# Wide products, fewer TensorE instructions: a two-layer decode kernel on one Trainium2 core

## Chip, cores and metric

The kernel runs on one core of one Trainium2 chip. The metric is the device time of one execution in microseconds. Times are given as the median of several runs; the profile comes from one further execution.

## What is computed

Two layers run one after the other over the same weights. Each layer is a decode step of grouped-query attention over a key and value cache, and then a gated feed-forward block; both have a layernorm ahead and a residual sum behind. There are 4 batch rows of 512 numbers, 32 query heads on 8 key/value heads, 4096 cached positions with 128 numbers a head, and a hidden width of 1792. All numbers are f32.

```python
def _A_ref(x, k_cache, v_cache, wq, wo):          # B, Sq, D = 4, 1, 512; 32 heads on 8
    q = (x @ wq).reshape(B, Sq, Hq, Dh).transpose(0, 2, 1, 3)
    k = jnp.repeat(k_cache, rep, axis=1)
    v = jnp.repeat(v_cache, rep, axis=1)
    p = softmax(einsum("bhqd,bhkd->bhqk", q, k) * Dh ** -0.5)
    o = einsum("bhqk,bhkd->bhqd", p, v)
    return o.transpose(0, 2, 1, 3).reshape(B, Sq, Hq * Dh) @ wo

def _B_ref(x, w1, w3, w2):
    h = silu(x @ w1) * (x @ w3)
    return h @ w2

for layer in range(2):
    x = x + _A_ref(layernorm(x), k_cache, v_cache, wq, wo)
    x = x + _B_ref(layernorm(x), w1, w3, w2)
```

## The kernel before, in words

Every layer reads the whole cache, 64 MB of keys and 64 MB of values, so the program is mostly a stream of loads. The order of the loads is a list made ahead (`plan`, lines 120 to 187), and a small allocator gives each load a place in one large on-chip tile, `space`. `pump` (L192) issues the next loads of the list, all on SyncE's queue, as long as a place is free. `done` and `vacate` (L231, L240) return a place once TensorE has used what lay there, and call `pump` again. So a load is issued when TensorE has consumed something that came much earlier, and the loads land in the order of the list.

The attention walks over 16 steps in a layer: 8 key/value heads ("groups"), each in two halves of 2048 positions. `score` (L351) multiplies q with 16 key blocks of 512 positions. `maximum` and `exponent` make the softmax of one half with its own maximum (VectorE, ScalarE). `turn` (L379) transposes the weights p. `weigh` (L403) multiplies them with the value tiles. The blocks of scores and values run on four separate groups of 32 output partitions: `ps[32 * b:32 * b + 32, :]`. The work is interleaved: the scores of the next half are issued before the values of this half.

At the end of a group, `finish` (L413) joins the two halves. `join_sums` (L395) makes the factors of the halves, two instructions at L425 add them up into `o` (128 partitions by 4 blocks of 128 columns, of which each row needs one), and `turn_o` (L429) turns the four blocks in four products with parts of the identity. `project_o` (L437) multiplies by the group's 512 rows of wo: for each of the 4 heads of the group, four products of 128 columns, each into its own 32 partitions of `x_ps`; L448 adds the result to the residual `x_sb`. `project_q` (L329) makes the next group's q the same way: four row blocks of wq times four heads, 16 products of 128 columns into `misc[32 * h:32 * h + 32, :]`, one VectorE scaling (L344), one transposition (L345) and two copies into `qT`.

A product of f32 numbers is two TensorE instructions with a weight load each, a transposition is one.

The residual is held as four blocks of 128 columns, each on the first 4 rows of its own 32 partitions, which is why the projections write their output in four parts.

At the end of a layer, the last group's projection is followed by `layernorm` (L302), the products with w1 and w3 (L466, L460), the gate (L471 to L478), the turning of the hidden vector (`turn_h`, L480), and `down` (L499), the products with the 14 row tiles of w2: for each tile four products of 128 columns into `x_ps` (L504). w2 arrives in seven loads (`W2_PARTS`, tiles 0-1, 2-5, 6-7, 8-9, 10-11, 12, 13). The sum is added to `x_sb` at L520 or, in the last layer, at L523, and L562 stores the output. Between these steps the kernel issues work for TensorE whose result nobody reads: `busy(n)` (L287) transposes the identity n times; the list `BUSY` says how often at which place.

Of the kernel before, what the change touches and what calls it, by code (L numbers as in the profile page):

```python
# [52 lines left out]


W2_PARTS = ((0, 2), (2, 6), (6, 8), (8, 10), (10, 12), (12, 13), (13, 14))
BUSY = (5, 3, 5, 3, 3, 4, 3, 2)
SCRATCH = 64


# [4 lines left out]
def tile_decode_layers(ctx: ExitStack, tc: tile.TileContext, x, kt, v, wqo, wo0, w1, w3, w2, out):  # L64
# [192 lines left out]

    alike = const.tile([P, P], F32, name="alike")
    block = const.tile([P, 2 * NB], F32, name="block")
    part = work.tile([P, 48], F32, name="part", tag="tmp", bufs=1)  # L260
    nc.vector.tensor_reduce(part[:, 0:16].rearrange("p (b h) -> p b h", b=B),
                            ident.rearrange("p (b j h) -> p b h j", b=B, h=REP), axis=AX.X, op=ALU.add)
    for j in range(2 * NB):
        nc.vector.tensor_copy(alike.rearrange("p (b j h) -> p b j h", b=B, h=REP)[:, :, j, :],
                              part[:, 0:16].rearrange("p (b h) -> p b h", b=B))
    nc.vector.tensor_reduce(part[:, 16:48].rearrange("p (b j) -> p b j", b=B),
                            ident.rearrange("p (b j h) -> p b j h", b=B, h=REP), axis=AX.X, op=ALU.add)
    nc.vector.tensor_reduce(block, part[:, 16:48].rearrange("p (b j) -> p j b", b=B), axis=AX.X, op=ALU.add)
    qT = const.tile([P, B, 32 + LEAD], F32, name="qT")
    nc.vector.memset(qT, 0.0)  # L270
    oT = const.tile([P, REP, B], F32, name="oT")
    hT = const.tile([P, 14, B], F32, name="hT")
    sums_ps = psum.tile([P, 2, P], F32, name="sums_ps")
    nc.vector.memset(sums_ps, 0.0)
    x_ps, misc = sums_ps[:, 0, :], sums_ps[:, 1, :]
    o_ps = [psum.tile([P, NB * DH], F32, name=f"o{i}", tag=f"o{i}") for i in range(STEPS)]
    for i in range(STEPS):
        nc.vector.memset(o_ps[i], 0.0)

    def scores():  # L280
        return psum.tile([P, BLOCK], F32, name="scores", tag="scores")
# [4 lines left out]

    def busy(n):  # L287
        if n:
            pt = scores()
            for i in range(n):  # L290
                nc.tensor.transpose(pt[:, 0:P], ident, ident)  # L291

    def small(name, bufs=1):
        return work.tile([P, 1], F32, name=name, tag=name, bufs=bufs)
# [31 lines left out]
        return xT, rstd, factor  # L326


    def project_q(layer, g, xT, rstd, factor=None):  # L329
        w = place(at_wq(g), HOME).rearrange("p (k n) -> p k n", k=KC)  # L330

        def product(k):
            for h in range(REP):
                nc.tensor.matmul(misc[32 * h:32 * h + 32, :], xT[:, 32 * k:32 * k + 32],  # L334
                                 w[:, k, h * DH:(h + 1) * DH], start=(k == 0), stop=(k == KC - 1))

        for k in range(KC):
            product(k)
            if factor and k == 1:
                factor()  # L340
        if layer:
            vacate(at_wq(g))
        q = work.tile([P, DH], F32, name="q", tag="tmp", bufs=1)
        nc.vector.tensor_scalar(q, misc, rstd, SCALE, op0=ALU.mult, op1=ALU.mult)  # L344
        nc.tensor.transpose(misc, q, ident)  # L345
        for at in (LEAD, LEAD + ROW):
            nc.vector.tensor_copy(qT[:, :, at:at + REP],
                                  misc.rearrange("p (h b) -> p b h", h=REP)[:, 0:B, :])


    def score(layer, g, c):  # L351
# [43 lines left out]
    def join_sums(acc):  # L395
        nc.vector.tensor_tensor(acc[:, 8:10], acc[:, 2:4], acc[:, 4:6], op=ALU.mult)
        nc.vector.tensor_tensor(acc[:, 10:11], acc[:, 8:9], acc[:, 9:10], op=ALU.add)  # L397
        nc.tensor.matmul(misc[:, 8:9], alike, acc[:, 10:11], start=True, stop=True)  # L398
        nc.vector.reciprocal(acc[:, 11:12], misc[:, 8:9])
        nc.vector.tensor_scalar(acc[:, 12:14], acc[:, 4:6], acc[:, 11:12], 2.0, op0=ALU.mult, op1=ALU.mult)  # L400


    def weigh(layer, g, c, i, pT):  # L403
# [6 lines left out]
            done("v", layer, g, c, r)  # L410


    def finish(layer, g, c, i, p, acc, after=None):  # L413
        pT = turn(p)
        if i < STEPS - 1:
# [7 lines left out]
        for j in (0, 2):  # L423
            s = slice(j * DH, (j + 2) * DH)
            nc.vector.scalar_tensor_tensor(o[:, s], o_ps[1][:, s], acc[:, 13:14], o[:, s], op0=ALU.mult,  # L425
                                           op1=ALU.add)
        return o

    def turn_o(o):  # L429
        for j in range(NB):  # L430
            own = ident.rearrange("p (b j h) -> p b j h", b=B, h=REP)[:, :, j, :]
            nc.tensor.matmul(misc[:, 0:B * REP], o[:, j * DH:(j + 1) * DH], own,  # L432
                             start=(j == 0), stop=(j == NB - 1))
        nc.vector.tensor_copy(oT, misc[:, 0:B * REP].rearrange("p (b h) -> p h b", b=B))


    def project_o(layer, g, rowsum):  # L437
        w = place(at_wo(g), HOME) if g or layer == 0 else loaded("wo", layer)
        w = w.rearrange("p (h e) -> p h e", h=REP)
        for h in range(REP):  # L440
            for k in range(KC):
                nc.tensor.matmul(x_ps[32 * k:32 * k + B, :], oT[:, h, :], w[:, h, k * P:(k + 1) * P],  # L442
                                 start=(h == 0), stop=(h == REP - 1))
        if layer and g == 0:
            done("wo", layer)
        elif layer or g == 0:
            vacate(at_wo(g))
        nc.vector.scalar_tensor_tensor(x_sb, x_ps, 1.0, x_sb, op0=ALU.mult, op1=ALU.add,  # L448
                                       accum_out=rowsum)

    def feed_forward(layer, xT, rstd, factor, rowsum):
        pg = o_ps[0]
# [46 lines left out]
        def down():  # L499
            for i, (a, b) in enumerate(W2_PARTS):  # L500
                t = loaded("w2", layer, a).rearrange("p (n e) -> p n e", n=b - a)
                for m in range(a, b):
                    for k in range(KC):
                        nc.tensor.matmul(x_ps[32 * k:32 * k + B, :], hT[:, m, :],  # L504
                                         t[:, m - a, k * P:(k + 1) * P], start=(m == 0), stop=(m == 13))
# [21 lines left out]
    for layer in range(LAYERS):  # L527
        xT, rstd, factor = layernorm(x_sb, rowsum)
        steps = orders[layer]
        project_q(layer, steps[0][0], xT, rstd, factor)  # L530
        accs, before = {}, None
        for n, (g, c) in enumerate(steps):
            i = n % STEPS
            if i == 0:
                accs[g] = work.tile([P, 16], F32, name="acc")
            ps = score(layer, g, c)
            maximum(i, ps, accs[g])
            if n == 0:
                p = exponent(i, ps, accs[g])
            elif i == 0:  # L540
                o = finish(layer, *before, p, accs[before[0]])
                turn_o(o)
                p = exponent(i, ps, accs[g])
            else:
                if n > 1:
                    project_o(layer, steps[n - 2][0], small("rowsum"))
                p = finish(layer, *before, p, accs[g], (i, ps, accs[g]))
# [12 lines left out]
        rowsum = small("rowsum")  # L560
        feed_forward(layer, xT, rstd, factor, rowsum)
# [45 lines left out]
```

## Time and profile before

| | |
|---|---|
| median of 3 runs | 711.88 us (711.68 to 711.91) |
| the profiled execution | 712.09 us |
| its span, first to last instruction | 710.2 us |
| granted TensorE clock, mean | 0.817 |
| loads | 299.18 MB, 16 DMA engines busy 99.1% of the span |
| TensorE instructions | 3994 matmuls and 3994 weight loads |

The profile shows one execution. An instruction's row has its start and duration, its engine (PE is TensorE, PEld its weight loads, DVE VectorE, ACT ScalarE, POOL GpSimd, SPq the issuing of loads by SyncE), its line, what it writes and reads, its shape and how many of the same kind were merged into the row (x32). Brackets give the idle time of the engine ahead of it and what ended that. The chain of waits is followed back from the last instruction, at each step to what released it. Matmuls overlap, so a row of several is read by the starts of the rows around it rather than by summing durations.

### The profile page before, as it was taken

To read this page: it belongs to the slowest core of one execution; us is meant where nothing else is said; L and a number is where in the kernel's file an instruction comes from. 1 tells how busy PE (TensorE), PEld (TensorE's weight loads), DVE (VectorE), ACT (ScalarE), POOL (GpSimd) and SP (SyncE) were. 2 spreads that over 40 slices of the span, in tenths; PEclk is the share of its full clock that TensorE was granted. 3 is DMA by queue.
4 is the path that set the end of the run, shared out by engine and by line. 5 is a ranking of instruction groups with operands and counts; after the bars stand their busy time and mean duration, and the time that the engine had idled before them with its cause. 6 is when DMAs were issued, how large, how long until landed. Compare 5 with 4: busy or idle time off the path is not lost.

```text
span 710.2 us, 8882 instructions
## 1 busy us (share of the span) xinstructions
PE 452.9 (64%) x3994; PEld 166.2 (23%) x3994; DVE 106.5 (15%) x372; ACT 42.3 (6%) x101; POOL 2.9 (0%) x10
## 2 busy tenths in 40 slices
PE   4542766367662666675687766576566686666887
PEld 2111222122211222121234211122122222222234
DVE  2011011011110111111211110110111111111121
ACT  0000000000000000010111100000000000000011
POOL 0000000000000000000000000000000000000000
PEclk8687687677976889799999988886888867787799
DMA  9999999999999999999999999999999999999996
GB/s 374 434 436 431 426 435 429 430 433 427 435 430 432 433 427 429 434 418 418 420 419 408 412 426 429 428 433 432 430 435 425 431 437 420 438 426 424 426 417 257
DMA packets 19477, 299.80 MB, mean 422 GB/s; under 512 B 2160, under 2 KB 2416, under 8 KB 6384
## 3 DMA queue, kind: packets, MB, share of 16 engines
q1 hardware_dynamic: 19296, 299.18, 99.1%
q8 instruction: 31, 0.51, 0.3%
q10 hardware_dynamic: 144, 0.07, 0.0%
q14 instruction: 6, 0.05, 0.0%
HBM read 299.17 MB, written 0.07 MB: 421 GB/s over the span
## 4 chain that ended last, share of the span: by engine, by line
DMA 83%; PE 15%; DVE 1%; issue 1%; SPq 0%; ACT 0%; POOL 0%; ACTq 0%
DMA space<-in_v 47%; DMA space<-in_kt 28%; DMA space<-in_w 8%; PE scores L361 6%; PE o L408 6%; PE sums_ps L442 0%; PE scores L291 0%; PE sums_ps L334 0%; ACT p L375 0%; DVE acc L371 0%; SPq L213 0%; PE o L460 0%; SPq L201 0%; PE sums_ps L432 0%; PE sums_ps L504 0%
## 5 line engine op out<-in xcount | busy, mean ns | idle before, releaser
L408 PE MATMUL o<-space,pT 128*16 128x512 f32 x1024 | 170.1, 806 | 128.6 <-DMA space<-in_v 127.0
L361 PE MATMUL scores<-space,qT 128*32 128x512 f32 x1024 | 157.2, 763 | 81.0 <-DMA space<-in_kt 75.0
L408 PEld LDWEIGHTS o<-space,pT 128*16 128x16 f32 x1024 | 32.6, 117 | 235.2 <-issue 141.3
L361 PEld LDWEIGHTS scores<-space,qT 128*32 128x32 f32 x1024 | 41.0, 134 | 173.2 <-issue 140.6
L371 DVE TENSOR_REDUCE acc<-scores 128x1 f32<-128x512 f32 x32 | 22.1, 692 | 231.1 <-PE scores L361 231.1
L375 ACT ACTIVATE p<-scores,acc 128x512 f32<-128x512 f32 x32 | 22.0, 687 | 456.9 <-PE sums_ps L432 297.9
L425 DVE SCALAR_TENSOR_TENSOR o<-o,acc,o 128x256 f32<-128x256 f32 x32 | 14.0, 479 | 129.9 <-PE o L408 129.9
L392 DVE TENSOR_REDUCE acc<-sums_ps 128x1 f32<-128x8 f32 x16 | 2.7, 166 | 142.8 <-PE sums_ps L391 142.8
L432 PE MATMUL sums_ps<-ident,o 128*128 128x16 f32 x128 | 17.0, 265 | 8.6 <-DVE o L425 8.6
L334 PE MATMUL sums_ps<-space,xT 128*32 128x128 f32 x512 | 19.2, 294 | 3.7 <-DVE acc L392 3.6
L432 PEld LDWEIGHTS sums_ps<-ident,o 128*128 128x128 f32 x128 | 15.5, 191 | 25.3 <-DVE o L425 25.1
L382 PE MATMUL turned<-ident,p 128*128 128x128 f32 x128 | 21.0, 286 | 0.0
L442 PE MATMUL sums_ps<-space,oT 128*4 128x128 f32 x512 | 17.7, 280 | 0.0
L382 PEld LDWEIGHTS turned<-ident,p 128*128 128x128 f32 x128 | 13.6, 142 | 16.9 <-issue 16.0
L442 PEld LDWEIGHTS sums_ps<-space,oT 128*4 128x4 f32 x512 | 14.2, 90 | 10.1 <-issue 9.4
L291 PE MATMUL scores<-ident 128*128 128x128 f32 x80 | 14.6, 300 | 1.4 <-POOL ident masks.py:199 1.4
L334 PEld LDWEIGHTS sums_ps<-space,xT 128*32 128x32 f32 x512 | 13.9, 117 | 5.7 <-DVE acc L392 4.9
L398 PE MATMUL sums_ps<-acc,alike 128*128 128x1 f32 x32 | 6.1, 261 | 13.0 <-DVE acc L397 13.0
L384 DVE COPY pT<-turned 128x256 f32<-128x256 f32 x32 | 13.4, 419 | 4.3 <-PE turned L382 4.3
L393 ACT ACTIVATE acc<-acc 128x2 f32<-128x2 f32 x16 | 4.7, 296 | 144.6 <-DVE acc L392 144.6
L421 DVE TENSOR_SCALAR o<-o,acc 128x512 f32<-128x512 f32 x16 | 12.0, 751 | 0.6
L291 PEld LDWEIGHTS scores<-ident 128*128 128x128 f32 x80 | 9.5, 151 | 6.4 <-issue 4.9
(78 smaller groups left out, 141.5 us busy)
## 6 DMA issues: line engine op xcount, KB each, us to landing
space<-in_kt SPq DMA_DIRECT2D x23, 4096.0 KB, 28.3
space<-in_v SPq DMA_DIRECT2D x22, 4096.0 KB, 32.3
space<-in_v SPq DMA_DIRECT2D x11, 2048.0 KB, 22.0
space<-in_kt SPq DMA_DIRECT2D x9, 2048.0 KB, 19.7
space<-in_v SPq DMA_DIRECT2D x14, 1024.0 KB, 19.8
space<-in_wqo SPq DMA_DIRECT2D x3, 4096.0 KB, 42.7
space<-in_kt SPq DMA_DIRECT2D x7, 1024.0 KB, 11.8
space<-in_w SPq DMA_DIRECT2D x6, 1024.0 KB, 17.2
```

The source lines that it names most:

```text
L291: nc.tensor.transpose(pt[:, 0:P], ident, ident)
L334: nc.tensor.matmul(misc[32 * h:32 * h + 32, :], xT[:, 32 * k:32 * k + 32], w[:, k, h * DH:(h + 1) * DH], start=(k == 0), stop=(k == KC - 1))
L361: nc.tensor.matmul(ps[32 * b:32 * b + 32, :], qT[:, b, at:at + 32], t[:, i * BLOCK:(i + 1) * BLOCK], start=(m < 2), stop=(m >= TILES - 2))
L371: nc.vector.tensor_reduce(acc[:, i:i + 1], ps, axis=AX.X, op=ALU.max, negate=True)
L375: nc.scalar.activation(p.rearrange("p n s -> p (n s)"), ps, AF.Exp, bias=acc[:, i:i + 1], accum_out=acc[:, 2 + i:3 + i])
L382: nc.tensor.transpose(pt[:, n, :], p[:, n, :], ident)
L384: nc.vector.tensor_copy(pT, pt.rearrange("p n (b r) -> p n b r", b=B)[:, :, :, 0:ROW])
L408: nc.tensor.matmul(o_ps[i][32 * b:32 * b + ROW, :], pT[:, r // 2, b, :], t[:, j * NB * DH:(j + 1) * NB * DH], start=(r < 2), stop=(r >= TI ...
L421: nc.vector.tensor_scalar(o, o_ps[0], acc[:, 12:13], None, op0=ALU.mult)
L425: nc.vector.scalar_tensor_tensor(o[:, s], o_ps[1][:, s], acc[:, 13:14], o[:, s], op0=ALU.mult, op1=ALU.add)
L432: nc.tensor.matmul(misc[:, 0:B * REP], o[:, j * DH:(j + 1) * DH], own, start=(j == 0), stop=(j == NB - 1))
L442: nc.tensor.matmul(x_ps[32 * k:32 * k + B, :], oT[:, h, :], w[:, h, k * P:(k + 1) * P], start=(h == 0), stop=(h == REP - 1))
```

## The change

The parts of the change are:

- `project_q` uses, for all groups but a layer's first, four products of 512 columns into the first 32 partitions of a tile `wide` (the whole bank of `sums_ps`) in place of 16 products of 128 columns. The scaling becomes four instructions, one for each head. In the first group of a layer the order changes: `factor`, which makes rstd, is issued ahead of all products instead of after half of them. One copy into `qT` replaces two.
- `project_o` does the same for all groups but a layer's last: four products of 512 columns into 4 rows of `wide`. The result is added to the residual by `add_rows`, four VectorE instructions of 4 rows by 128 columns, which `finish` issues after the transposed weights were copied.
- The end of a group: `o` has one block of 128 columns instead of four. `join_sums` makes eight factors, one for each half and block, which are zero where a row doesn't own the block; one scaling and seven additions of 128 columns gather `o`. Four of these additions stand after the second half's values. `turn_o` is one product.
- `down`: the first ten tiles of w2 use one product of 512 columns each, into 4 rows of `sides[0]`; `add_rows` adds them to the residual. The last four tiles stay as they were.
- `busy(n)` issues one product of n times 128 columns in place of n transpositions, and the counts go from 5, 3, 5, 3, 3, 4, 3, 2 to 4, 3, 4, 3, 0, 4, 3, 2.

Matmuls and weight loads together go from 7988 to 6148.

```diff
-BUSY = (5, 3, 5, 3, 3, 4, 3, 2)
+WIDE = 10
+BUSY = (4, 3, 4, 3, 0, 4, 3, 2)
...
+    head = const.tile([P, B * REP], F32, name="head")
...
-    sums_ps = psum.tile([P, 2, P], F32, name="sums_ps")
+    sums_ps = psum.tile([P, KC, P], F32, name="sums_ps")
...
+    wide = sums_ps.rearrange("p k c -> p (k c)")
...
     def busy(n):
         if n:
-            pt = scores()
-            for i in range(n):
-                nc.tensor.transpose(pt[:, 0:P], ident, ident)
+            pt = scores().rearrange("p (k c) -> p k c", k=KC)
+            nc.tensor.matmul(pt[:, 0:n, :], ident, ident.unsqueeze(1).to_broadcast([P, n, P]),
+                             start=True, stop=True)
...
+        if factor:
+            factor()
         for k in range(KC):
-            product(k)
-            if factor and k == 1:
-                factor()
+            if factor:
+                for h in range(REP):
+                    nc.tensor.matmul(misc[32 * h:32 * h + 32, :], xT[:, 32 * k:32 * k + 32],
+                                     w[:, k, h * DH:(h + 1) * DH], start=(k == 0), stop=(k == KC - 1))
+            else:
+                nc.tensor.matmul(wide[0:32, :], xT[:, 32 * k:32 * k + 32], w[:, k, :],
+                                 start=(k == 0), stop=(k == KC - 1))
...
+            for h in range(REP):
+                nc.vector.tensor_scalar(q[32 * h:32 * h + 32, :], wide[0:32, h * DH:(h + 1) * DH],
+                                        rstd[0:32, :], SCALE, op0=ALU.mult, op1=ALU.mult)
...
+        nc.vector.tensor_tensor(acc[:, 16:24].rearrange("p (i j) -> p i j", i=2),
+                                block[:, 0:NB].unsqueeze(1).to_broadcast([P, 2, NB]),
+                                acc[:, 12:14].unsqueeze(2).to_broadcast([P, 2, NB]), op=ALU.mult)
...
-        o = work.tile([P, NB * DH], F32, name="o", tag="p", bufs=1)
-        nc.vector.tensor_scalar(o, o_ps[0], acc[:, 12:13], None, op0=ALU.mult)
+        o = work.tile([P, DH], F32, name="o", tag="p", bufs=1)
+        nc.vector.tensor_scalar(o, o_ps[0][:, 0:DH], acc[:, 16:17], None, op0=ALU.mult)
+
+        def add(s, js):
+            for j in js:
+                nc.vector.scalar_tensor_tensor(o, o_ps[s][:, j * DH:(j + 1) * DH], acc[:, 16 + NB * s + j:17 + NB * s + j],
+                                               o, op0=ALU.mult, op1=ALU.add)
+
+        add(0, range(1, NB))
         weigh(layer, g, c, i, pT)
...
+        add(1, range(NB))
...
     def turn_o(o):
...
+        nc.tensor.matmul(misc[:, 0:B * REP], o, head, start=True, stop=True)
...
+            if rowsum is None:
+                nc.tensor.matmul(wide[0:B, :], oT[:, h, :], w[:, h, :], start=(h == 0), stop=(h == REP - 1))
...
+    def add_rows(a):
+        for k in range(KC):
+            rows = x_sb[32 * k:32 * k + B, :]
+            nc.vector.tensor_tensor(rows, a[0:B, k * P:(k + 1) * P], rows, op=ALU.add)
...
+                    if m < WIDE:
+                        nc.tensor.matmul(sides[0][0:B, :], hT[:, m, :], t[:, m - a, :],
+                                         start=(m == 0), stop=(m == WIDE - 1))
...
+                if b == WIDE:
+                    add_rows(sides[0])
```

More of the change, by code (lines that the diff above doesn't have):

```diff
@@ L259, in tile_decode_layers @@
     block = const.tile([P, 2 * NB], F32, name="block")
-    part = work.tile([P, 48], F32, name="part", tag="tmp", bufs=1)
-    nc.vector.tensor_reduce(part[:, 0:16].rearrange("p (b h) -> p b h", b=B),
+    head = const.tile([P, B * REP], F32, name="head")
+    part = work.tile([P, 32], F32, name="part", tag="tmp", bufs=1)
+    nc.vector.tensor_reduce(head.rearrange("p (b h) -> p b h", b=B),
                             ident.rearrange("p (b j h) -> p b h j", b=B, h=REP), axis=AX.X, op=ALU.add)
@@ L410, in weigh, with finish @@
             done("v", layer, g, c, r)
-    def finish(layer, g, c, i, p, acc, after=None):
+    def finish(layer, g, c, i, p, acc, after=None, projected=False):
         pT = turn(p)
+        if projected:
+            add_rows(wide)
         if i < STEPS - 1:
@@ L419, in finish, with project_o @@
         join_sums(acc)
-        o = work.tile([P, NB * DH], F32, name="o", tag="p", bufs=1)
-        nc.vector.tensor_scalar(o, o_ps[0], acc[:, 12:13], None, op0=ALU.mult)
+        o = work.tile([P, DH], F32, name="o", tag="p", bufs=1)
[5 more added lines that the diff above has]
+        add(0, range(1, NB))
         weigh(layer, g, c, i, pT)
[L423 to L426, printed above, removed]
+        add(1, range(NB))
         return o
     def turn_o(o):
[L430 to L433, printed above, removed]
+        nc.tensor.matmul(misc[:, 0:B * REP], o, head, start=True, stop=True)
         nc.vector.tensor_copy(oT, misc[:, 0:B * REP].rearrange("p (b h) -> p h b", b=B))
-    def project_o(layer, g, rowsum):
+    def project_o(layer, g, rowsum=None):
         w = place(at_wo(g), HOME) if g or layer == 0 else loaded("wo", layer)
@@ L440, in project_o @@
         for h in range(REP):
-            for k in range(KC):
-                nc.tensor.matmul(x_ps[32 * k:32 * k + B, :], oT[:, h, :], w[:, h, k * P:(k + 1) * P],
-                                 start=(h == 0), stop=(h == REP - 1))
+            if rowsum is None:
+                nc.tensor.matmul(wide[0:B, :], oT[:, h, :], w[:, h, :], start=(h == 0), stop=(h == REP - 1))
+            else:
+                for k in range(KC):
+                    nc.tensor.matmul(x_ps[32 * k:32 * k + B, :], oT[:, h, :], w[:, h, k * P:(k + 1) * P],
+                                     start=(h == 0), stop=(h == REP - 1))
         if layer and g == 0:
@@ L447, in project_o @@
             vacate(at_wo(g))
-        nc.vector.scalar_tensor_tensor(x_sb, x_ps, 1.0, x_sb, op0=ALU.mult, op1=ALU.add,
-                                       accum_out=rowsum)
+        if rowsum is not None:
+            nc.vector.scalar_tensor_tensor(x_sb, x_ps, 1.0, x_sb, op0=ALU.mult, op1=ALU.add,
+                                           accum_out=rowsum)
+    def add_rows(a):
+        for k in range(KC):
+            rows = x_sb[32 * k:32 * k + B, :]
+            nc.vector.tensor_tensor(rows, a[0:B, k * P:(k + 1) * P], rows, op=ALU.add)
     def feed_forward(layer, xT, rstd, factor, rowsum):
@@ L534, in tile_decode_layers @@
             if i == 0:
-                accs[g] = work.tile([P, 16], F32, name="acc")
+                accs[g] = work.tile([P, 24], F32, name="acc")
             ps = score(layer, g, c)
@@ L545, in tile_decode_layers @@
                 if n > 1:
-                    project_o(layer, steps[n - 2][0], small("rowsum"))
-                p = finish(layer, *before, p, accs[g], (i, ps, accs[g]))
+                    project_o(layer, steps[n - 2][0])
+                p = finish(layer, *before, p, accs[g], (i, ps, accs[g]), n > 1)
                 join_maxima(accs[g])
```

29 lines of the change are left out of this document (14 added, 15 removed).

## The prediction

> **What bounds the kernel now.** I read the page first (its parts 1, 3, 4, 5 and 6), then the chain of waits in order of time, the DMA queues in two stretches, and the timeline of the end of each layer.
>
> ```profile
> span 710.2 us, 8882 instructions
> ...
> PE 452.9 (64%) x3994; PEld 166.2 (23%) x3994; DVE 106.5 (15%) x372; ACT 42.3 (6%) x101; POOL 2.9 (0%) x10
> ...
> PEclk8687687677976889799999988886888867787799
> ...
> q1 hardware_dynamic: 19296, 299.18, 99.1%
> q8 instruction: 31, 0.51, 0.3%
> ...
> L408 PE MATMUL o<-space,pT 128*16 128x512 f32 x1024 | 170.1, 806 | 128.6 <-DMA space<-in_v 127.0
> L361 PE MATMUL scores<-space,qT 128*32 128x512 f32 x1024 | 157.2, 763 | 81.0 <-DMA space<-in_kt 75.0
> ...
> space<-in_kt SPq DMA_DIRECT2D x23, 4096.0 KB, 28.3
> ```
>
> The loads fill all 16 DMA engines for 99.1% of the span, and TensorE stands idle 128.6 + 81.0 us ahead of its two big groups, nearly all of it waiting for loads. So one stream of 299 MB sets the time, and TensorE's work counts in two places only: behind the last load, and where it gives room to the stream too late. A 4 MB load takes about 9.7 us of the stream (below) and lands 28.3 us after its issue, so it is usually issued some 18 us early.
>
> ```profile
> 523.63 25.33 DMA space<-in_kt
> 554.92 32.90 DMA space<-in_kt
> 593.12 34.80 DMA space<-in_kt
> 696.31 10.66 DMA space<-in_w
> 707.48 0.29 DVE x_sb L523
> ```
>
> The chain's rows give landings: 548.96, 587.82, 627.92, and the last weight at 706.97, half a microsecond ahead of the final addition. Between the first two landings lie four loads, 38.86 us or 9.71 each; between the next two again four, but 40.10: 1.24 us are lost.
>
> ```profile
> q8 instruction: 24, 0.39, 0.3%
> ```
> ```profile
> q8 instruction: 26, 0.43, 0.3%
> ```
>
> These are the instruction queue's packets up to 587.82 and up to 627.92. By the page it moves 31 packets of some 16 KB for 7988 TensorE instructions (matmuls and weight loads), one for each 258. Packets 25 and 26 fall into the slow four loads. A packet occupies one DMA engine, and a load is done when its slowest engine is; other packets cost nothing visible, so I read it as a round over the engines, in which the first packet of each new round sets all later landings back.
>
> **What a wide product costs.** All products here are f32 in two instructions.
>
> ```profile
> 692.11 0.39 PE L308 MATMUL turned<-same,rowsum 128*128 128x128 f32 x2
> 692.33 0.49 PE L291 MATMUL scores<-ident 128*128 128x128 f32 x3
> ...
> 701.93 1.06 PE L504 MATMUL sums_ps<-space,hT 128*4 128x128 f32 x32
> ```
> ```profile
> 389.44 0.15 PEld L361 LDWEIGHTS scores<-space,qT 128*32 128x32 f32 x4 [0.28 <-issue]
> 389.87 0.16 PEld L361 LDWEIGHTS scores<-space,qT 128*32 128x32 f32 x4 [0.27 <-issue]
> ```
>
> Two instructions of 128 columns on the whole array follow one another in 0.22 us, 0.11 each. The 32 of L504, also 128 columns but on four separate groups of 32 output partitions, take 1.06 with the drain: four run in the time of one. Four of 512 columns on the four groups (L361) take 0.43. The changed products write 512 columns to one group: the other three stand empty, and each product takes 2 x 0.43 = 0.86, where before four products took 2 x 0.11 = 0.22 together. The change halves and halves again the count of instructions, and multiplies TensorE's time by four.
>
> **Inside the layers.** A q and an o projection go from 1.06 to 4 x 0.86 = 3.4 us each: 2 x 14 x 2.4 = 67 us more, less some 0.7 for each turned output. q's scaling becomes four VectorE instructions in a row, about 1 us more ahead of the next scores; the four row additions of an o product are issued behind pT's copy and only delay VectorE. I cost all that at nothing: it is covered by the 209.6 us of idle time and the 18 us lead. Gone is the cover only where the lead is short.
>
> **The instruction stream.** 920 fewer matmuls and as many loads leave 6148, and 6148 / 258 = 23.8: at most 24 packets, so the setback that begins with packet 25 is gone: 1.24 us; with the smaller one that I allow for packet 27, 1.5 us earlier landings.
>
> **The end of the layer, twice.** Behind the last value tile TensorE runs one chain to the end.
>
> ```profile
> 687.90 0.77 PE L291 MATMUL scores<-ident 128*128 128x128 f32 x5
> 688.02 0.88 DVE L425 SCALAR_TENSOR_TENSOR o<-o,acc,o 128x256 f32<-128x256 f32 x2 [5.88 <-PE o L408]
> 688.56 1.06 PE L432 MATMUL sums_ps<-ident,o 128*128 128x16 f32 x8
> ...
> 689.93 1.06 PE L442 MATMUL sums_ps<-space,oT 128*4 128x128 f32 x32
> 690.92 0.77 PE L291 MATMUL scores<-ident 128*128 128x128 f32 x5
> ...
> 698.48 0.66 PE L291 MATMUL scores<-ident 128*128 128x128 f32 x4
> 698.98 0.38 PE L484 MATMUL turned<-ident,gate 128*128 128x128 f32 x2
> ...
> 700.35 0.62 PE L504 MATMUL sums_ps<-space,hT 128*4 128x128 f32 x16
> ...
> 705.74 1.67 PE L504 MATMUL sums_ps<-space,hT 128*4 128x128 f32 x32 [0.22 <-DMA space<-in_w]
> ```
>
> The output's four additions of 128 columns, each on the result of the one before, cost between 0.88 (as two of 256) and 1.76 (as four of these); 1.3 I take. The one product that turns it takes about 0.35 where eight instructions took 1.06: together no change. The idle work is dearer: a transposition is one instruction (0.11), an idle product two passes over all columns: 0.86 for four blocks instead of 0.43 to 0.55, 0.64 for three instead of 0.33. The first is hidden by VectorE. The one ahead of the o product costs 0.35, the next 0.3, the third 0.2 beyond ScalarE's copy, the two around L484 0.4 and 0.3: w2 begins at 701.9 instead of 700.35. From there: two wide tiles 1.72; turning the second part of h and an idle product 1.07; four tiles 3.44; idle 0.43; two tiles 1.72; idle 0.43; two tiles 1.72; idle 0.43; the four narrow tiles 0.86 and the drain 0.2: 12.0, so 713.9 for the last addition instead of 707.48. The new row additions (about 1.2 us on VectorE, from 712.5) end just before it. **6.4 us more**, all behind loads that have landed: no cover. Ten tiles are 2.6 MB, 6.2 us at the stream's 299 MB in 705 us, and now take 8.6.
>
> In layer 0 the same work stands ahead of layer 1, and there the stream's lead is short.
>
> ```profile
> 376.25 0.62 PE L504 MATMUL sums_ps<-space,hT 128*4 128x128 f32 x16 [0.33 <-DMA space<-in_w]
> ...
> 384.28 0.29 DVE L520 SCALAR_TENSOR_TENSOR x_sb<-sums_ps,x_sb 128x128 f32<-128x128 f32 x1 [6.47 <-PE sums_ps L504]
> ...
> 387.36 0.33 SPq L211 DMA_DIRECT2D space<-in_kt  x1
> 387.84 0.35 DVE L344 TENSOR_SCALAR q<-sums_ps,rstd 128x128 f32<-128x128 f32 x1 [0.73 <-POOL rstd L324]
> ...
> 389.01 2.35 PE L361 MATMUL scores<-space,qT 128*32 128x512 f32 x20 [0.44 <-DVE qT L347]
> 390.10 1.19 SPq L213 DMA_DIRECT2D space<-in_v  x2
> ```
> ```profile
> space<-in_wqo SPq DMA_DIRECT2D x1, 1024.0 KB, 5.3
> space<-in_kt SPq DMA_DIRECT2D x1, 256.0 KB, 7.2
> out<-x_sb SPq DMA_DIRECT2D x1, 64.0 KB, 1.5
> ```
>
> Loads bound the first half there, so w2 begins at 376.4. The same 12.0 gives 388.4 for L520, 4.1 later. The following idle products add 0.3; moving rstd's products ahead of q's (q's then stand behind their wait for the sum of squares, which by the same shifts is there when the idle product ends) takes 0.4 off the wait of L344 for GpSimd, one copy fewer 0.1: the first scores start at 392.9, 3.9 late. They free the room for the loads issued at 390.10, behind which the whole stream queues. The load before them, issued at 387.36, lands 7.2 later, at 394.56: a lead of 4.46 shrinks to 0.55. What a queue that has run dry needs from issue to flow, this trace doesn't show; bounds are the 64 KB store (1.5, of which 0.15 is moving) and the very first load (5.3 less 2.5 for 1 MB at the stream's rate, 2.8). Between 1.4 and 2.8 I take 2.1: **1.5 us of dry stream**, with ends 0.8 and 2.3, and 0 if the delay comes out one or two microseconds smaller. The Trainium skill (DMA: Bandwidth & Descriptors, Anatomy of one DMA, written for the software path) has a fixed cost of about 2.0 us; the stall by it is an estimated 1.45, and no row here shows it for a load.
>
> **Sum.** The profiled execution took 712.09 us (span 710.2 and 1.9 around it): 712.09 + 6.4 + 1.5 - 1.5 = 718.5. The three runs' median is 711.88, 0.2 less: 718.3.
>
> **Rivals.**
> *Wide products are free.* If an instruction of 512 columns on one group took about what one of 128 takes, all that grew above would shrink below its loads; only the saved packets count: 711.9 - 1.5 = 710.4. Against it stand the 0.43 us of L361; for it only that no row shows 512 columns alone on the array. It decides below 0.3 us an instruction (ten tiles in the loads' 6 us). The Trainium skill (TensorE: Matmul & The Clock Gate, Back-to-back issue gap) gives sustained spacings of 81 ns at 128 columns and 131 ns at 512, by which wide products would win; L361's spacing disagrees. Chance 0.12.
> *No dry stream:* the delay at 389.01 is under 2.4 us, or a load flows within 0.55: 716.8. Chance 0.25.
> *The packets' setback stays,* since it hangs on something else: 719.8. Chance 0.14.
> *The clock drops* for products that use one group with four columns: 20 wide w2 instructions at double 0.43 add 8.6: 727. The row of the granted clock has slices of 6 tenths, but where TensorE waits for loads; its last two, in which the chain runs, have 9. Chance 0.05.
> The forecast has 0.44.
>
> **How the numbers follow.** About 0.2% (1.4 us) can be told from no change. The free rival lies at that bound, 0.08 faster and 0.04 same; all else is slower, 0.88. The range 714.5 to 721.5 takes in the forecast, the dry-stream and packet cases, and 2 us of error in the chain.
>
> **What would show it.** In the profile after: w2's wide group at 0.43 us spacing; L523's counterpart some 6 to 7 us behind the last landing instead of 0.5; 24 packets on the instruction queue; a gap in the stream around 392 to 396; layer interiors unmoved. I am wrong if w2's tiles still wait for loads, or if more than 3 us of TensorE's time inside the layers shows up as a stream that runs dry.

## The result, and the profile after

| | before | after |
|---|---|---|
| median | 711.75 us (711.64 to 711.91, 6 runs) | 724.15 us (722.98 to 724.43, 6 runs) |
| the profiled execution | 712.09 us | 722.98 us |
| its span | 710.2 us | 721.2 us |

The change makes the kernel slower: ratio 1.017, interval 1.0157 to 1.0183, or 12.4 us. The forecast was 718.3, so the direction was right and the size about half: 6.4 us of slowing down instead of 12.4, and the time lies above the range of the prediction. The profiled execution is the shortest of the six; what follows explains its 722.98 and can say little on the 1.2 us between it and the median.

First the page of the changed kernel: span, busy time of the engines, the granted clock in 40 slices, the load queue and the instruction queue, and the two big groups with their idle time.

```profile
span 721.2 us, 7201 instructions
...
PE 504.4 (70%) x3074; PEld 147.6 (20%) x3074; DVE 155.2 (22%) x530; ACT 42.4 (6%) x101; POOL 2.9 (0%) x10
...
PEclk8787698788987988899999999989898969899999
...
q1 hardware_dynamic: 19296, 299.18, 97.7%
q8 instruction: 24, 0.39, 0.2%
...
L421 PE MATMUL o<-space,pT 128*16 128x512 f32 x1024 | 143.2, 695 | 83.9 <-DMA space<-in_v 77.0
L371 PE MATMUL scores<-space,qT 128*32 128x512 f32 x1024 | 158.1, 770 | 60.1 <-DMA space<-in_kt 52.1
```

TensorE has 920 matmuls fewer and is busy 51.5 us longer. The idle time ahead of the two groups shrank from 209.6 to 144.0 us: the wide q and o products went into it. 24 packets came for 31. The last slices of the clock are 9, as before. The loads fill 97.7% of the span instead of 99.1%: 16.6 us are left without them instead of 6.4. Most of that is a longer end, 8.1 us by the rows below; some 2 us are left for a place at which the stream runs short.

Next the timeline of the end of the changed kernel.

```profile
690.78 1.13 PE L294 MATMUL scores<-ident 128*128 128x512 f32 x2
...
705.36 1.88 PE L530 MATMUL o<-space,hT 128*4 128x512 f32 x4
...
708.30 3.60 PE L530 MATMUL o<-space,hT 128*4 128x512 f32 x8
711.82 0.70 PE L294 MATMUL scores<-ident 128*128 128x256 f32 x2
712.45 1.88 PE L530 MATMUL o<-space,hT 128*4 128x512 f32 x4
714.26 0.70 PE L294 MATMUL scores<-ident 128*128 128x256 f32 x2
...
718.46 0.29 DVE L555 TENSOR_TENSOR x_sb<-sums_ps,x_sb 128x128 f32<-128x128 f32 x1 [0.48 <-PE sums_ps L534]
```

The first row is the idle product behind the last value tile. It starts 2.88 us later than in the kernel before (687.90): so much later does the stream deliver. The last addition comes 10.98 later (707.48): the other 8.10 us are the chain from the one row to the other, 27.68 instead of 19.58. No load is waited for in it. The two parts, 2.9 of stream and 8.1 of chain, are the whole difference of the profiled executions, 10.9.

The stream runs short at the border between the layers. These are the stretches of 3 us of the kernel before (busy time and count of PE, PEld, DVE, ACT and POOL, granted clock, DMA share, GB/s):

```profile
386.00:389.00 3.00, 1.52 (x42) 1.03 (x42) 0.77 (x4) 1.67 (x4) 0.55 (x1) 1.00 1.01 403
389.00:392.00 3.00, 2.99 (x28) 1.11 (x32) 0.00 (x0) 0.00 (x0) 0.00 (x0) 1.00 0.96 367
392.00:395.00 3.00, 1.39 (x16) 0.29 (x12) 0.69 (x1) 0.78 (x2) 0.00 (x0) 1.00 1.04 410
395.00:398.00 3.00, 3.00 (x29) 0.81 (x22) 0.00 (x0) 0.00 (x0) 0.00 (x0) 1.00 1.02 429
```

And of the changed one:

```profile
386.00:389.00 3.00, 3.00 (x35) 1.22 (x36) 1.13 (x4) 0.00 (x0) 0.00 (x0) 1.00 0.91 329
389.00:392.00 3.00, 3.00 (x44) 1.46 (x36) 0.89 (x5) 0.28 (x1) 0.00 (x0) 1.00 0.84 288
392.00:395.00 3.00, 2.17 (x45) 1.11 (x41) 0.70 (x3) 1.57 (x3) 0.55 (x1) 1.00 0.82 288
395.00:398.00 3.00, 2.68 (x28) 0.57 (x20) 0.25 (x1) 0.00 (x0) 0.00 (x0) 1.00 0.66 197
```

The last column lacks 74, 79, 122 and 232 GB/s for 3 us each, 1.52 MB together; at the stream's 424 GB/s that is 3.6 us. The measure is rough, since the stretch ahead of these lacks 90 too (329 for 419) and loses nothing in the landings; step 2 below goes by the landings.

### The profile page after: what moved, and what is told of

The parts are those of the page before. It is cut to its first block, busy times and chain, and to the rows that moved or that the text cites. A ratio compares the mean times of both kernels' runs of the same rounds, so it can differ in the third digit from the quotient of the medians.

```text
span 721.2 us, 7201 instructions
## 1 busy us (share of the span) xinstructions
PE 504.4 (70%) x3074; PEld 147.6 (20%) x3074; DVE 155.2 (22%) x530; ACT 42.4 (6%) x101; POOL 2.9 (0%) x10
## 3 DMA queue, kind: packets, MB, share of 16 engines
q1 hardware_dynamic: 19296, 299.18, 97.7%
## 4 chain that ended last, share of the span: by engine, by line
DMA 67%; PE 30%; DVE 2%; issue 1%; SPq 0%; ACT 0%; DVEq 0%
DMA space<-in_kt 48%; DMA space<-in_v 17%; PE scores L371 12%; PE o L421 6%; PE sums_ps L458 4%; PE o L530 2%; DMA space<-in_w 2%; PE scores L294 2%; PE sums_ps L345 2%; PE o L486 1%; PE turned L392 1%; DVE q L353 1%; DVE pT L394 0%; PE o L492 0%; PE sums_ps L534 0%
## 5 line engine op out<-in xcount | busy, mean ns | idle before, releaser
L421 PE MATMUL o<-space,pT 128*16 128x512 f32 x1024 | 143.2, 695 | 83.9 <-DMA space<-in_v 77.0
L440 DVE SCALAR_TENSOR_TENSOR o<-o,acc,o 128x128 f32<-128x128 f32 x112 | 39.3, 351 | 93.5 <-PE o L421 90.1
L345 PE MATMUL sums_ps<-space,xT 128*32 128x512 f32 x112 | 50.7, 595 | 3.6 <-DVE acc L402 3.6
L458 PE MATMUL sums_ps<-space,oT 128*4 128x512 f32 x112 | 50.5, 594 | 0.0
L353 DVE TENSOR_SCALAR q<-sums_ps,rstd 32x128 f32<-32x128 f32 x56 | 19.1, 341 | 52.6 <-PE sums_ps L345 52.0
L294 PE MATMUL scores<-ident 128*128 128x384 f32 (+2 forms) x48 | 23.3, 569 | 1.4 <-POOL ident masks.py:199 1.4
L449 PE MATMUL sums_ps<-head,o 128*128 128x16 f32 x32 | 6.3, 273 | 24.0 <-DVE o L440 24.0
L355 PE MATMUL sums_ps<-ident,q 128*128 128x128 f32 x16 | 5.2, 328 | 22.1 <-DVE q L353 21.0
L530 PE MATMUL o<-space,hT 128*4 128x512 f32 x40 | 18.5, 592 | 0.0
L475 DVE TENSOR_TENSOR x_sb<-sums_ps,x_sb 4x128 f32<-4x128 f32 x56 | 15.6, 279 | 0.6
```

What stands on the lines that cost most here:

```text
L294: nc.tensor.matmul(pt[:, 0:n, :], ident, ident.unsqueeze(1).to_broadcast([P, n, P]), start=True, stop=True)
L345: nc.tensor.matmul(wide[0:32, :], xT[:, 32 * k:32 * k + 32], w[:, k, :], start=(k == 0), stop=(k == KC - 1))
L353: nc.vector.tensor_scalar(q[32 * h:32 * h + 32, :], wide[0:32, h * DH:(h + 1) * DH], rstd[0:32, :], SCALE, op0=ALU.mult, op1=ALU.mult)
L421: nc.tensor.matmul(o_ps[i][32 * b:32 * b + ROW, :], pT[:, r // 2, b, :], t[:, j * NB * DH:(j + 1) * NB * DH], start=(r < 2), stop=(r >= TI ...
L440: nc.vector.scalar_tensor_tensor(o, o_ps[s][:, j * DH:(j + 1) * DH], acc[:, 16 + NB * s + j:17 + NB * s + j], o, op0=ALU.mult, op1=ALU.add)
L458: nc.tensor.matmul(wide[0:B, :], oT[:, h, :], w[:, h, :], start=(h == 0), stop=(h == REP - 1))
```

## The experiments

Every kernel here computes the whole of the reference; some add idle work. Times are medians, each compared with the kernel before on the same chip.

**Attention alone.** The changed kernel with the old end: only the attention part is left, that is the wide q and o products, the gathered output with its one turning product, and the earlier factor.

```diff
-WIDE = 10
-BUSY = (4, 3, 4, 3, 0, 4, 3, 2)
+WIDE = 0
+BUSY = (5, 3, 5, 3, 3, 4, 3, 2)
...
-            pt = scores().rearrange("p (k c) -> p k c", k=KC)
-            nc.tensor.matmul(pt[:, 0:n, :], ident, ident.unsqueeze(1).to_broadcast([P, n, P]),
-                             start=True, stop=True)
+            pt = scores()
+            for i in range(n):
+                nc.tensor.transpose(pt[:, 0:P], ident, ident)
```

> The change's attention part alone: wide q and o products inside the layers, one product to turn a group's output, rstd's products first; idle work and w2 as before. Theory (TensorE's work counts only at the two layer ends): all of this is hidden behind the loads, so 710.5 to 712.2 us, at most a microsecond off 711.75, by the packets of the instruction queue that go (about 26 are left of 31). Rival (67 us more TensorE work inside the layers starves the stream somewhere): 714 us or more, with gaps between landings inside the layers.

Measured: 711.89 us (711.61 to 712.11, 10 runs), ratio 1.0003 (0.9994 to 1.0012): no change. The wide projections are hidden, but no packet's gain is seen either. Its profile says why. From its page, its chain of waits, the DMA queues between 703 and 705 us, and the timeline of the end:

```profile
q8 instruction: 25, 0.41, 0.2%
...
556.02 31.69 DMA space<-in_kt
594.46 32.10 DMA space<-in_kt
```
```profile
q8 instruction: 1, 0.02, 3.4%
```
```profile
704.06 0.62 PE L534 MATMUL sums_ps<-space,hT 128*4 128x128 f32 x16 [0.21 <-DMA space<-in_w]
706.36 1.16 PE L534 MATMUL sums_ps<-space,hT 128*4 128x128 f32 x16 [1.67 <-DMA space<-in_w]
```

The two key loads land at 587.71 and 626.56, 38.85 us apart; before it was 40.10. So the setback has gone from there. But this kernel still has a packet 25, and it comes at 703.87, among the last loads: the 256 KB load that L534 waits for at 706.36 lands 2.20 us behind the one before it, where 0.66 is usual. The 1.5 us were moved to the end, not saved.

**w2 alone.** The kernel before with the part of the change in `down` (ten tiles in one product each, and the four row additions), all else untouched.

> The kernel before with only w2's first ten tiles in wide products, idle work and attention as before. Theory: the chain behind the last value tile grows by 4.8 us (ten tiles at 0.86 us against loads that bring one in 0.61, after work that was already level with the loads), and the first scores of layer 1 start 3.9 us later, which leaves the stream dry for about 2 us: 718.5. Rival (the idle products and the switches around them are the larger part): 715 or less.

Measured: 720.18 us (718.47 to 721.67, 4 runs), ratio 1.0119 (1.01 to 1.0138). From the timeline of its end:

```profile
691.94 0.77 PE L292 MATMUL scores<-ident 128*128 128x128 f32 x5
...
704.39 1.88 PE L505 MATMUL o<-space,hT 128*4 128x512 f32 x4
...
716.38 0.29 DVE L532 TENSOR_TENSOR x_sb<-sums_ps,x_sb 128x128 f32<-128x128 f32 x1 [0.22 <-PE sums_ps L509]
```

w2 begins 12.45 us behind the last value tile, as before, and then takes 11.99 to the last addition instead of 7.13. That is 4.9 us. The stream adds 4.0: the first row starts 4.04 later than before (687.90). The 718.5 that were expected are missed by 1.7: I had put the dry stream at about 2.

**Idle work alone.** The kernel before with the new `busy` and its new counts.

> The kernel before with only the idle work in wide products (and the new counts). Theory: w2 begins 2.0 us later, as it did after the change (12.45 us behind the last value product before, 14.48 after), and each of the three idle products between w2's loads adds 0.25; part of that is hidden by the wait for w2's loads, so the last addition is 1.5 us later; the boundary moves by 1.5 to 2 us, at the edge of what its lead covers: 713.3. Rival (idle work only fills waits): 711.8.

Measured: 713.53 us (713.39 to 713.68, 8 runs), ratio 1.0026 (1.0016 to 1.0036). From the timeline of its end:

```profile
687.60 1.13 PE L290 MATMUL scores<-ident 128*128 128x512 f32 x2
...
702.02 0.62 PE L504 MATMUL sums_ps<-space,hT 128*4 128x128 f32 x16
```

w2 begins 14.42 behind the last value tile: the wide idle products cost 1.97 ahead of it. From there w2 takes 6.95 to the last addition at 708.97, since its tiles wait for loads.

**The whole change with the old idle work.**

```diff
 WIDE = 10
-BUSY = (4, 3, 4, 3, 0, 4, 3, 2)
+BUSY = (5, 3, 5, 3, 3, 4, 3, 2)
```

with `busy` as in the first experiment.

> The whole change but for the idle work, which is as before. Theory: attention part free, w2 part as in the run with w2 alone: 718.0, and 6 us under the whole change, of which 3 lie behind the last load and up to 3 in a stream that runs dry less. Rival (w2 alone costs nearly all): 722 or more.

Measured: 718.39 us (717.9 to 721.84, 5 runs), ratio 1.0094 (1.0077 to 1.0111). So the wide idle products cost some 5.5 us (the difference of the two ratios) in the company of the wide w2 tiles, where alone they cost 1.8: the parts don't add up. The chain behind the last value tile takes 24.78 here (692.50 to 717.28) and 27.68 in the whole change, so 2.9 of the 5.5 stand there; alone, inside w2, the idle work still hides below loads. Where the rest lies isn't shown: this profile is of the slowest of the five executions (721.84), and its stream is later than that of the whole change (692.50 against 690.78).

**Fewer instructions still.** The first experiment's kernel, in which the layernorm's four narrow products with `same` are one with four copies of it side by side.

```diff
+    same4 = const.tile([P, P], F32, name="same4")
+    for k in range(KC):
+        nc.vector.tensor_copy(same4[:, 32 * k:32 * k + 32], same)
...
-        for k in range(KC):
-            nc.tensor.matmul(out[32 * k:32 * k + 32, :], same, part, start=True, stop=True)
+        nc.tensor.matmul(out, same4, part, start=True, stop=True)
```

> The attention part alone (which gave 711.89 us), and besides the means of the layernorms in one product of 128 output rows instead of four of 32: 96 TensorE instructions fewer, 6427 instead of 6523 with its waits. In the attention run packet 25 of the instruction queue came at 703.87 us, after 6454 instructions, and set back the landing of a small w2 load by 1.54. Theory (packets 1, 9, 17 and 25 each set the stream back once): packet 25 no longer falls before the last load, the last load lands at about 705.4, and the time is 710.3 us, below both kernels. Rival (the setback near the end had another cause): 711.8, with the last landing near 707 again.

Measured: 710.32 us (710.13 to 710.74, 11 runs), ratio 0.998 (0.9971 to 0.9989). It beats both kernels. The end of its chain of waits, and its instruction queue between 704.6 and 704.8 us:

```profile
694.93 10.68 DMA space<-in_w
...
706.13 0.29 DVE x_sb L557
```
```profile
q8 instruction: 1, 0.02, 29.9%
```

Packet 25 has moved from 703.87 to between 704.6 and 704.8. The last weight lands at 705.62 and the last addition follows at 706.13, 1.35 earlier than in the kernel before. 96 instructions fewer than in the first experiment moved one packet by less than a microsecond and saved 1.6 (711.89 to 710.32): the packet's place decides, not the instructions' own time.

**More packets.** The kernel before with 27 idle transpositions ahead of the q products of 14 groups, in time in which TensorE waits for loads.

```diff
                 if n + 1 < len(steps):
+                    busy(27)
                     project_q(layer, steps[n + 1][0], xT, rstd)
```

> The kernel before with 27 idle transpositions more in each of 14 groups, ahead of q's products, where TensorE waits for loads: 756 TensorE instructions more, 34 packets instead of 31, so that packet 33 falls well before the last load. Theory (packets 1, 9, 17, 25 and then 33 set the stream back): one more setback, 713.0 to 713.4. Rival (the number of instructions has no price of its own, and the work is hidden): 711.8. If the work itself weren't hidden, 14 times 2.9 us could be lost in part, and landings would show gaps in every group.

Measured: 713.19 us (712.67 to 713.5, 11 runs), ratio 1.0018 (1.001 to 1.0027). From its page, and its chain of waits:

```profile
q8 instruction: 34, 0.56, 0.3%
...
696.18 12.20 DMA space<-in_w
```

Its landings are set back five times, by 1.51 to 1.54 us, at packets 1, 9, 17, 25 and 33; the kernel before has four, at packets 1, 9, 17 and 25, each in two pieces: 1.2 to 1.3 there, and 0.3 two packets later. Number 33 comes at 696.6, and the next w3 load lands 1.53 late. The last weight lands at 708.38 instead of 706.97. Together with the kernel above, a round of eight packets is shown from both sides for a stream that doesn't run dry: one setback more costs 1.4 us, one less saves 1.4.

**Either layer's end alone.** The changed kernel with a switch that puts the idle work and w2's tiles of one layer's end back to the old form.

```diff
+            n_wide = WIDE if end["wide"] else 0
...
-                    if m < WIDE:
+                    if m < n_wide:
...
+        if layer:
+            end["wide"] = False
```

(for layer 0's end alone wide; the other kernel has the two values exchanged.)

> The change with the end of layer 1 as before: w2 narrow and idle transpositions there; the wide w2 and the wide idle products stay at the end of layer 0. Theory: layer 1's first scores start 5 us later, the stream runs dry for 3 to 3.5 us around 390 to 399, as in the profile of the change, and the end costs nothing: 714 to 716. Rival (a dry stream at the boundary is made up for later, because the loads are in advance again): 712 or less.

Measured: 716.19 us (715.49 to 717.6, 4 runs), ratio 1.0065 (1.0051 to 1.0079), so 4.4 us.

> The change with the end of layer 0 as before, and the wide w2 and idle products at the end of layer 1 alone. Theory: no dry stream at the boundary; the last addition stands 27.6 us behind the last value product instead of 19.6, 8.0 more, and the stream itself is 0 to 1.5 earlier by the packets: 718.3 to 719.8. Rival (the chain behind the last load costs the 6.4 us of the prediction and the boundary the rest): 717 or less.

Measured: 718.85 us (718.44 to 719.36, 4 runs), ratio 1.01 (1.0086 to 1.0114), so 7.1 us. From the timeline of the latter, the first idle product behind the last value tile and the last addition:

```profile
686.16 1.13 PE L301 MATMUL scores<-ident 128*128 128x512 f32 x2
...
713.82 0.29 DVE L563 TENSOR_TENSOR x_sb<-sums_ps,x_sb 128x128 f32<-128x128 f32 x1 [0.49 <-PE sums_ps L542]
```

With a stream that never runs dry the chain takes 27.66, just as in the whole change, and starts 1.74 us *earlier* than in the kernel before (687.90): here the saved setback is kept. So the two ends are separate losses, 4.4 + 7.1 = 11.5 of the 12.4.

**A delay between the layers.** The kernel before with idle transpositions behind layer 0's last addition, which hold everything that follows, nothing else.

```diff
                                            accum_out=rowsum)
+            busy(18)
```

> The kernel before with 18 more idle transpositions (2.0 us) at the end of layer 0 ahead of the layernorm. The lead of the loads issued at 390.10 falls from 4.46 to about 2.5 us. In the run with 36 a lead of 0.2 cost 2.7 us. Theory (a load flows about 3 us after its issue): dry for 0.5, so 712.0 to 712.6. Rival (the loss grows with the delay from the first microsecond, as the stream has no reserve at all): 713 or more.

Measured: 712.02 us (711.84 to 712.74, 10 runs), ratio 1.0004 (0.9995 to 1.0013).

The same with `busy(36)`:

> The kernel before with 36 more idle transpositions (3.9 us at 0.11) at the end of layer 0 ahead of the layernorm, and nothing else changed. It measures what a late release costs by itself. Theory: the lead of the loads issued at 390.10 falls from 4.46 to about 0.55, and a load needs 2.4 to 3 us from its issue until it flows, so the stream is dry for 2 to 3 us: 713.8 to 714.8. The prediction's price was 1.5: 713.3. Rival (a queue needs no lead of its own): 711.8.

Measured: 714.37 us (713.99 to 716.61, 4 runs), ratio 1.0043 (1.003 to 1.0057). From its stretches of 3 us:

```profile
389.00:392.00 3.00, 2.25 (x55) 1.73 (x54) 0.86 (x5) 1.58 (x4) 0.55 (x1) 1.00 0.72 291
392.00:395.00 3.00, 2.26 (x21) 0.95 (x25) 0.50 (x3) 0.27 (x1) 0.00 (x0) 1.00 0.46 157
```

The lead of a load is the time from its issue to the landing of the load ahead of it. Two microseconds of delay leave the loads leads of 2.2 and 2.7 us and cost at most 0.9; two more leave one of them a lead of 0.2, and it lands 2.7 late. So the price has a threshold, as the prediction had it, but past it 2.6 us are lost (by the medians).

## Why the prediction was right in direction and too low

The prediction's sum for a profiled execution was 718.5, and 722.98 came. The chain to the end was put 1.7 too low (step 1), the layer border 1.9 too low (step 2), and of the 1.5 that the packets were to win back 1.0 did not come (step 3).

**What held.** A wide product costs what L361's spacing said: the eight instructions at 708.30 take 3.52 us, 0.44 each. The rival of free products fell by that, and the clock rival by the last slices of 9. The interior is hidden: attention alone changes nothing. The chance of 0.88 for slower rested on these.

**Step 1, the chain to the end: predicted 6.4, measured 8.1.** The two experiments on its parts place the error:

| | last value tile to w2 | w2 to last addition |
|---|---|---|
| before | 12.45 | 7.13 |
| w2 alone | 12.45 | 11.99 |
| idle work alone | 14.42 | 6.95 |
| the change | 14.58 | 13.10 |
| predicted | 14.0 | 12.0 |

Ahead of w2 the change costs 2.13 where I had 1.55. The idle work alone gives 1.97. The kernel with the old idle work takes 12.80 there (692.50 to 705.30), 0.35 more than the kernel before: that is the attention part, whose output and turning product I had put at no change. Inside w2 the rows of the timeline above exceed my terms one by one: 2.94 instead of 2.79 up to 708.30, 3.52 instead of 3.44 for four tiles, 1.81 instead of 1.72 for each of two pairs of tiles (712.45 to 714.26), and 0.63 instead of 0.43 for each of three idle products of 256 columns (711.82 to 712.45). So the largest of the mis-sized terms is the idle work, about 0.8 of the 1.7: three times 0.2 inside w2, where I had put four passes of 0.11, and some 0.2 ahead of it. The kernel before had the same surcharge in view, in its timeline:

```profile
702.91 0.44 PE L291 MATMUL scores<-ident 128*128 128x128 f32 x2
703.28 0.62 PE L504 MATMUL sums_ps<-space,hT 128*4 128x128 f32 x16
```

Two transpositions between narrow products take 0.37, where 0.22 is the price in a row of the same kind. I took 0.11 per pass from a row of whole-array products and used it between narrow ones. Each passage between a product on the whole array and one on 32 output partitions costs about 0.1 us (0.15 and 0.20 for there and back). The Trainium skill (TensorEngine Tiling (Array Packing), Key Properties) says that a change of tiling mode drains TensorE; it gives no number, and these rows agree with it. That the surcharge is this drain was not tried by itself.

**Step 2, the layer border: predicted 1.5 (0.8 to 2.3), measured about 3.4.** The delay of the first scores was to be 3.9 and is 5.0 (389.01 to 394.04), by the same rows inside w2. The larger error is the step "the load before them, issued at 387.36, lands 7.2 later": I held that load in its place and delayed only the ones at 390.10. But everything that L504 and the q products release moves with them. From the timeline, SyncE's issues; before:

```profile
382.02 2.57 SPq L213 DMA_DIRECT2D space<-in_v  x3
```

and after:

```profile
387.71 2.01 SPq L215 DMA_DIRECT2D space<-in_v  x3
...
392.94 0.33 SPq L213 DMA_DIRECT2D space<-in_kt  x1
395.13 2.08 SPq L215 DMA_DIRECT2D space<-in_v  x3
```

The three value loads at 382.02 come 5.7 later, the small one at 387.36 comes 5.6 later, and those at 390.10 come 5.0 later. The issues of the changed kernel (KB, and us from issue to landing), for the loads issued at 385.27, 387.71, 388.92, 392.94 and 395.13:

```profile
space<-in_kt SPq DMA_DIRECT2D x1, 512.0 KB, 4.4
...
space<-in_v SPq DMA_DIRECT2D x1, 512.0 KB, 3.5
...
space<-in_v SPq DMA_DIRECT2D x1, 512.0 KB, 5.5
...
space<-in_kt SPq DMA_DIRECT2D x1, 256.0 KB, 3.3
...
space<-in_v SPq DMA_DIRECT2D x1, 512.0 KB, 3.6
```

They land at 389.7, 391.2, 394.4, 396.2 and 398.7. A load of 512 KB takes 1.24 us of the stream. The second is issued 2.0 us before the first has landed and comes 0.3 late; the third 2.3 before the second has, and comes 1.9 late; the last 1.1 before the fourth has, and comes some 1.2 late. Three places lose 3.4 us together where I had looked at one. Why a lead of 2.3 loses 1.9 here, when 2.2 lost next to nothing in the kernel with 18 idle transpositions, stays open. In the kernel with w2 alone even a lead of 3.6 lost 2.1 (a load of 1 MB, issued at 394.61, landed at 402.80, 4.6 behind the one ahead of it, where 2.5 is its share of the stream). So a lead isn't priced by its length alone, and the prediction's threshold holds only for a plain delay.

**Step 3, the packets: predicted 1.5 gained, 0.4 to 0.5 left.** The setback that begins with packet 25 is gone from its place, as predicted. From the chain of waits of the changed kernel:

```profile
527.54 24.28 DMA space<-in_kt
...
558.99 31.74 DMA space<-in_kt
...
597.52 32.07 DMA space<-in_kt
...
642.16 42.58 DMA space<-in_v
```

The landings are 551.82, 590.73, 629.59 and 684.74. Against the kernel before the first three are 2.86, 2.91 and 1.67 late: between the second and the third 1.24 us are won back. But the last values follow 2.86 late again, by their two rows of before and after:

```profile
681.92 6.05 PE L408 MATMUL o<-space,pT 128*16 128x512 f32 x32 [1.03 <-DMA space<-in_v]
```
```profile
684.78 6.07 PE L421 MATMUL o<-space,pT 128*16 128x512 f32 x32 [1.05 <-DMA space<-in_v]
```

So another setback lies between 629.59 and 684.74. The instruction queue has moved 20 packets up to the one and 22 up to the other. It is packet 22 that brings the setback, not 25; it comes at 670.4 us. The load issued at 635.73, in the changed kernel's issues:

```profile
space<-in_v SPq DMA_DIRECT2D x1, 2048.0 KB, 39.2
```

That load lands at 674.9, 1.5 late. Before it packet 14 comes at 417.8, and the load that lands at 420.1 is 0.9 late, after one at 409.3 that is 0.6 late with no packet of this queue near it. So behind the border the changed kernel is set back by 3.0 us; the kernel before is set back there by 3.1 (1.3 and 0.3 at packets 17 and 19, 1.2 and 0.3 at 25 and 27). Nothing was gained there. What is left of the gain lies ahead of the border, where the load that lands at 389.7 landed at 390.1 before.

The step that failed is that the round is counted from the first packet of the program. After the border it seems to be counted anew: 14 and 22 are eight apart. The kernel with the old idle work, which lost time at the border as well, has its setbacks of 1.5 at packets 14 and 22 again, and the kernel with w2 alone has 1.2 and 1.5 at packets 20 and 28. The kernel with only layer 1's end wide has no dry stretch, and its chain starts 1.74 earlier. My reading is that the dry stretch, in which all engines wait, lets the ones that lag catch up and so starts the round of eight anew. Against a clean proof stands the kernel with only layer 0's end wide, where smaller setbacks of 0.5 and 0.9 come at packets 17 and 21. The cause is argued, not shown. The Trainium skill (Runtime: NRT & Kernel Launch, Instruction fetch mechanics) has 16 KiB blocks of 256 instructions and calls the cost of crossing one mostly hidden. Here it isn't hidden once in a round of eight, and then costs a full stream 1.5 us.

**The sum made again** is 712.09 + 8.1 + 3.4 - 0.5 = 723.1 against the 722.98 of the profiled execution. The 0.5 in it is what the border's 3.4 leaves above the 2.9 by which the stream is late, so the sum has to come out. The remaining 1.2 us to the median come without a profile. Of the rivals the one that kept the setback was right in its effect, though it had moved from packet 25 to 22.

## What to carry to other kernels

A product that uses one output group instead of four pays for every column; below a wall of loads that is free, and behind the last load it is the time. Before costing a delay at a border where a stream runs on short leads, list every load that the delayed work releases, and the lead of each, not only the one that looks critical. And fewer instructions pay by where the last refill falls, not by their count: here removing one setback gained 1.4 us, and moving it to the end gained nothing.

## What the runs showed of the hardware that was not expected

- Instruction refills delay a saturated stream of loads once in a round of eight packets, by 1.5 us: in one piece at packets 1, 9, 17, 25 and 33 of the kernel with more packets, in two pieces in the kernel before (1.2 to 1.3, and 0.3 two packets later). Behind a stretch in which the stream ran short the round was a new one: packets 14 and 22 in two kernels, 20 and 28 in a third.
- Kernels whose stream runs dry scatter: the change, w2 alone, the old idle work, layer 0's end and the delay by 36 transpositions range over 1.4 to 3.9 us in 4 to 6 runs each; the others over 0.3 to 0.9 in 4 to 11. Why was not tried.
- A load that is issued 0.2 us before the queue runs empty lands 2.7 us late; a lead of 2.2 us lost next to nothing in one kernel, 2.3 lost 1.9 in another, and 3.6 lost 2.1 in a third.
